# Moving 25 zero writes behind the load they stood ahead of, and six to another queue, in the last attention of a decode-step kernel

## The chip, the cores and the metric

The kernel runs on one core of a Trainium2 chip. HBM is the chip's main memory, SBUF the core's working memory; DMA transfers between them are issued by an engine's queue (SyncE's or GpSimd's here), and TensorE, VectorE and ScalarE compute. The time is the device time of one execution in microseconds (us), lower is better. Times below are medians of all executions of a kernel. Profile times count from the start of the profiled span, which is about 2 us shorter than the time of the same execution.

## The reference, cut to what matters

The program is the forward pass of attention, MLP, attention, MLP for one token, and its gradient (`jax.vjp`) for every input. Both attentions share their weights and KV cache, and so do both MLPs. Attention looks only at the last W = 4096 of 32768 cache rows:

```python
k = jnp.repeat(k_cache[:, :, Sk - W:, :], rep, axis=1)
v = jnp.repeat(v_cache[:, :, Sk - W:, :], rep, axis=1)
...
x = x + _A_ref(_layernorm(x), k_cache, v_cache, wq, wo)      # "A1"
x = x + _B_ref(_layernorm(x), w1, b1, w2)                    # "B2"
x = x + _A_ref(_layernorm(x), k_cache, v_cache, wq, wo)      # "A3"
x = x + _B_ref(_layernorm(x), w1, b1, w2)                    # "B4"
```

So the gradients of the two caches are zero in 28672 of 32768 rows. These zeros, 2 x 4 x 28672 x 128 values of two bytes, 58.7 MB, have to be written to HBM by the kernel; it does so in 112 writes of 512 KB. They depend on nothing and can go out at any time. A third of the 172 MB that the kernel moves are these zeros, and they are the kernel's filling material: put where the DMA would be idle, they are free.

## The kernel before: the parts that matter

The zero writes go out from SyncE's queue (`zeros`) or from GpSimd's (`bg_zeros`, which first copies one column of a named tile so that the writes don't start too early):

```python
def zeros(n):
    for _ in range(min(n, len(zero_jobs))):
        nc.sync.dma_start(zero_jobs.pop(0), zt[:])

def bg_zeros(n, after):
    if n:
        nc.gpsimd.tensor_copy(gate_t[:], after[:, 0:1])
    for _ in range(min(n, len(zero_jobs))):
        nc.gpsimd.dma_start(zero_jobs.pop(0), zt[:])
```

Of the 16 chunks of wo, nine are kept in SBUF and seven are streamed through NB = 6 buffers. All large loads go out from SyncE. The backward pass of an attention (`first` is true for A3, false for A1, the last attention to be differentiated) starts like this:

```python
def attn_bwd(g_col, g_bf, lname, sv, first, nxt):
    ...
    for c in range(NR, min(NO, NR + NB)):
        held[c] = wo_load(c)                    # six streamed chunks
    if first:
        bg_zeros(Z["A3c"], g_bf)
    else:
        zeros(Z["A1"])                          # 29 zero writes, SyncE
    late = list(range(NR, NO))
    ...                                         # (kept chunks; uses g_bf)
    def T(i):
        c = late[i]
        if c not in held:
            held[c] = wo_load(c)                # the seventh: needs a buffer back
        w = held[c]
        xpose(*nat_blocks(w[:, 1, :]), "a")     # 8 TensorE transposes, ScalarE copy
        nc.vector.tensor_tensor_reduce(...)     # VectorE: the chunk's other half
    def M(i, _):                                # 8 matmuls on chunk i
        ...
        if not first and i:
            nextprep()                          # small side jobs (GpSimd, TensorE)
    pipe(list(range(len(late))), T, M)
    if first:
        pre.extend(w2_load(c) for c in range(NB))
        bg_zeros(Z["A3d"], g_bf)
        fill(100, ["V"])
    else:
        after_stream()
    ...  # serial chain: do_p (dO), dP, dS, dq, the product with wq, layer norm
```

One of the side jobs writes the gradient of b1 out, and its row lies in the single buffer `kp`; the next user of that buffer is the copy `yr` of the row sums at the end of the serial chain:

```python
def rows_copy(bank, eng):
    yr = work.tile([P, 512], FP32, name="yr", tag="kp")
    ...
def db1_out():
    ...
    db_row = work.tile([NW2, P, 2], BF16, name="db_row", tag="kp", ...)
    ...
    nc.gpsimd.dma_start(out_7.rearrange(...), db_row[:]...)
```

The final stage computes the weight and cache gradients as outer products, 40 MB of writes from SyncE, with the remaining zeros strewn in:

```python
Z = dict(B2=3, A3=16, B4=[5, 2, 1, 2, 1, 2, 6], A3c=6, A3d=29, W1=3, A1=29)
...
run(6)
while jobs:
    zeros(1)
    run(9)
zeros(1000)
```

Of the kernel before, what the change touches and what calls it, by code (L numbers as in the profile page):

```python
# [23 lines left out]
def kernel(  # L24
# [102 lines left out]
# [3 lines that stand above are left out]
# [3 lines left out]
# [6 lines that stand above are left out]
# [120 lines left out]
    def fill(n, keys, how=None, six=False):  # L259
        for i in range(n):  # L260
            for k in keys:
                if xq[k]:
                    ap = xq[k].pop(0)
                    xpose(*nat_blocks(ap), None if how is None else how[i % len(how)], six)
                    break

    def level():
        ev[:] = [0.0, 0.0]
# [61 lines left out]
    def wo_load(c):  # L330
        if c < NR:
            w = wo_kept[c]
        else:
            w = strm.tile([P, 2, D], BF16, name="wo_c", tag="st")[:]
        nc.sync.dma_start(w, wo_v[c])
        return w

    def w2_load(c):
        w = strm.tile([P, 2, D], BF16, name="w2_c", tag="st")
        nc.sync.dma_start(w[:], w2_v[c])  # L340
        return w
# [25 lines left out]
    def pipe(items, T, M, lag=1):  # L367
        n = len(items)
        for i in range(n + lag):
            if i < n:  # L370
                T(items[i])
            if i >= lag:
                M(items[i - lag], i - lag)
# [46 lines left out]
    def attn_fwd(x_col, lname, first):  # L420
# [31 lines left out]
        if not first:  # L452
            for c in range(NR, min(NO, NR + NB)):
                held[c] = wo_load(c)
            bg_zeros(Z["A3"], n_bf)
            for w in wq_t:
# [130 lines left out]
    def w2_pass(a_bf, g_bf, x_col, xname, wgname, gbc, zn):  # L587

        acc = wide(TD + NW2)
        wg = keep.tile([P, NW2, 2], FP32, name=wgname)  # L590
        held = []

        def bwd1(w, c):
            for dch in range(TD):
                mv(acc, TD + c, w[:, 1, dch * P:(dch + 1) * P], g_bf[:, dch:dch + 1], False, dch == TD - 1)

        for c in range(NW2):
            w = pre.pop(0) if pre else w2_load(c)
            fwd_rows2(acc, w, c, a_bf, c == 0, c == NW2 - 1)
            ps = psum1([P, 8, P], BF16, "tps")  # L600
            for b in range(TD):
                nc.tensor.transpose(ps[:, b, :], w[:, 1, b * P:(b + 1) * P], ident_bf[:])  # L602
            nc.scalar.copy(w[:, 1, :], ps[:].rearrange("p b c -> p (b c)"))  # L603
            scr = work.tile([P, D], BF16, name="scr", tag="kp")
            nc.vector.tensor_tensor_reduce(out=scr[:], in0=w[:, 0, :], in1=gbc[:], scale=1.0, scalar=0.0,  # L605
                                           op0=ALU.mult, op1=ALU.add, accum_out=wg[:, c, 0:1])
            if held:
                bwd1(held.pop(), c - 1)
            if c == NW2 - 2 and zn:
                bg_zeros(zn, wg[:, c, :])  # L610
            held.append(w)
        bwd1(held.pop(), NW2 - 1)
        x_new = keep.tile([P, TD], FP32, name=xname)
        nc.vector.tensor_add(x_new[:], x_col[:], acc.cols(0, TD))
        nc.vector.tensor_copy(wg[:, :, 1:2], acc.cols(TD, TD + NW2)[:, :, None])
        return x_new, wg

    def mlp_fwd(x_col, lname, g_bf):
# [20 lines left out]
        sv["dact"] = dact  # L639
        x_new, wg = w2_pass(a_bf, g_bf, x_col, f"x_{lname}", "wg4", gbc, Z["B2"])  # L640
        return x_new, sv, wg
# [5 lines left out]
    def w1_block(b, hh):  # L647
        w = strm.tile([P, HT, CB], BF16, name="w1_b", tag="st")
        nc.sync.dma_start(w[:], w1_v[:, hh * HT:(hh + 1) * HT, b * CB:(b + 1) * CB])
        return w  # L650

    def mlp_turn(x_col, lname, wg, g_col, nxt):
# [22 lines left out]
        def lo0(b):  # L675
            return max(b - 1, 0) * FB
# [6 lines left out]
        for b in range(NBK):  # L683
            bg_zeros(Z["B4"][b], dh_bf[:, lo0(b):] if b else n_bf)
            ws[b] = [w1_block(b, hh) for hh in range(2)]
# [38 lines left out]
    def mlp_bwd_w1(g_col, lname, sv, nxt):  # L724
# [15 lines left out]
        level()  # L740
        bg_zeros(Z["W1"], sv["dh_bf"])
        pipe(list(range(2 * TD)), T, M)
        return ln_bwd(nacc.cols(0, TD), sv["n32"], sv["rstd"], g_col, lname, nxt)

    def attn_bwd(g_col, g_bf, lname, sv, first, nxt):
# [3 lines left out]
        held = {}  # L749
        for c in range(NR, min(NO, NR + NB)):  # L750
            held[c] = wo_load(c)
        if first:
            bg_zeros(Z["A3c"], g_bf)
        else:
            zeros(Z["A1"])
        late = list(range(NR, NO))
        gbc = bcast_row(g_bf)
        drow = sm_tile(P, 512)
# [42 lines left out]
# [3 lines that stand above are left out]
            fill(100, ["V"])  # L804
        else:
            after_stream()

        do_p = work.tile([P, 2, NO], BF16, name="do_p")
        dcols = dacc.cols(0, HQ).rearrange("p (c t) -> p t c", t=2)
# [242 lines left out]
    def after_stream():  # L1052
        slots.extend(strm.tile([P, 2048], BF16, name="st_o", tag="st")[:] for _ in range(NB))
# [9 lines left out]
        for _ in range(min(n, len(prep))):  # L1063
            prep.pop(0)()

    Z = dict(B2=3, A3=16, B4=[5, 2, 1, 2, 1, 2, 6], A3c=6, A3d=29, W1=3, A1=29)


    x1 = None
# [39 lines left out]
    x3, sA3 = attn_fwd(x2, "A3", False)  # L1109
    g3, g3b, sB4 = mlp_turn(x3, "B4", wg4, gcol, "A3")  # L1110
    g2, g2b = attn_bwd(g3, g3b, "A3", sA3, True, "B2")
    x4, wg2 = w2_pass(sB4["a_bf"], g2b, x3, "x_B4", "wg2", bcast_row(g2b), 0)
    dh_of(wg2, "B2", sB2)
# [4 lines left out]
    def db1_out():  # L1118
# [7 lines left out]
        nc.gpsimd.dma_start(out_7.rearrange("(c x) -> c x", x=2 * P), db_row[:].rearrange("c p t -> c (p t)"))  # L1126

    g0, g0b = attn_bwd(g1, g1b, "A1", sA1, False, "X0")
    level()
    nextprep(100)  # L1130
# [50 lines left out]
```

## Time and profile before

| | kernel before |
|---|---|
| time, median of the first 3 runs | 483.97 us (483.75 to 491.44) |
| span of the profiled run | 486.7 us |
| bytes moved | 172.23 MB, mean 354 GB/s |
| VectorE, ScalarE, TensorE busy | 49%, 46%, 67% |

The page cuts the span into 40 slices of 12.2 us. The rows are the granted TensorE clock in tenths (the share of full speed that the chip's throttle let TensorE run at), the busy share of the 16 DMA engines in tenths, and what they moved.

```profile
PEclk9996555587869998957987598855557555755555
DMA  8999999999999999999979999999000999999997
GB/s 328 387 415 419 407 370 383 342 359 392 413 375 396 350 307 377 415 417 417 414 291 310 329 342 339 416 420 417 26 1 3 393 413 403 413 413 409 421 415 301
```

The DMA is the limit nearly everywhere, but for three slices (26, 1 and 3 GB/s) in which it does nothing. The windows view, in microseconds, shows what stands on either side of that hole (columns: busy time and count for each engine, then granted clock, DMA share, GB/s):

```profile
310.00:320.00 10.00, 3.50 (x70) 2.96 (x67) 0.00 (x0) 6.20 (x8) 2.80 (x18) 0.85 1.03 417
320.00:330.00 10.00, 0.00 (x0) 0.00 (x0) 0.00 (x0) 0.00 (x0) 0.00 (x0) 0.50 1.03 421
330.00:340.00 10.00, 0.00 (x0) 0.00 (x0) 0.00 (x0) 0.00 (x0) 0.00 (x0) 0.50 1.02 419
345.00:376.00 31.00, 21.85 (x309) 12.63 (x309) 11.06 (x43) 7.16 (x11) 3.38 (x16) 0.67 0.01 2
```

First the DMA works for over 20 us while every engine is idle; then the engines work for 31 us while the DMA is idle. Two things that don't depend on each other run one after the other. (A DMA share of 1.03 is this view's full.) SyncE's queue in the timeline shows what ties them together (start, duration, queue, line, what, count):

```profile
299.33 32.66 SPq L129 DMA_DIRECT2D out_dram<-zt  x29
332.96 0.34 SPq L335 DMA_DIRECT2D wo_c<-in_A_wo_dram  x1
376.75 2.58 SPq L991 DMA_DIRECT2D out_dram<-wo_b  x3
```

and TensorE's and VectorE's first instructions after the hole say what they waited for, in brackets:

```profile
342.90 1.03 PE L186 MATMUL tps<-ident_bf,wo_c 128*128 128x128 bf16 x8 [28.15 <-DMA wo_c<-in_A_wo_dram]
343.02 1.22 DVE L784 CUSTOM_DVE_ANT_0 wo_c<-wo_c,gbc 128x1024 bf16<-128x1024 bf16 x1 [33.20 <-DMA wo_c<-in_A_wo_dram]
```

The seventh load was issued at 332.96 and landed 9.9 us later. Its buffer had been free since 308.8, when the last matmul that reads the old content ended,

```profile
308.45 0.36 PE L222 MATMUL acc<-gA_pair,wo_c 128*128 128x16 bf16 x8 [0.70 <-ACT wo_c L148]
```

but SyncE was working through the 29 zero writes that stand ahead of it in program order. The chain of waits, followed back from the end of the span, runs through just this:

```profile
311.85 0.96 SPq L129
...
312.85 10.05 DMA out_dram<-zt
...
322.92 9.97 DMA out_dram<-zt
...
332.96 9.89 DMA wo_c<-in_A_wo_dram
...
342.90 1.05 PE tps L186 x8
```

The last lines to keep for later are from the end of the serial chain, where the b1 row goes out and `yr` is copied:

```profile
367.86 0.51 POOL L1126 DMA_DIRECT2D out_dram<-db_row  x1 [12.38 <-DVE db_row L1125]
...
369.49 0.40 PE L222 MATMUL acc<-wq_b,dq_pair 128*32 128x512 bf16 x4
369.94 0.69 DVE L238 COPY yr<-acc 128x512 f32<-128x512 f32 x1 [2.38 <-PE acc L222]
370.69 1.05 PE L222 MATMUL sm<-sel,yr 128*128 128x2 f32 x8 [0.80 <-DVE yr L238]
```

The row lands in 1.6 us here, by the DMA view, and `yr` waits for TensorE alone.

### The profile page before, as it was taken

Reading aid. Unit: us, or ns where it says so; the run is one execution under the profiler, and the core shown is the slowest. Engines: PE = TensorE matmul, PEld = TensorE weight load, DVE = VectorE, ACT = ScalarE, POOL = GpSimd, SP = SyncE. Lnnn points to the kernel's source line nnn. Section 1 sums busy time; section 2 is a strip of 40 time slices with the busy share of each in tenths; the row PEclk is TensorE's granted clock in tenths of the full one; section 3 lists DMA queues with packets and bytes.
Section 4 is the critical chain, followed back from the end, with each engine's and each line's share of the span. In section 5 each row is a group of like instructions: output and inputs, shape, how many; then the busy total and the mean of one; then the engine's idle time right before and its main releaser. Section 6 shows DMA issues by size and latency. Waiting matters only on the chain.

```text
span 486.7 us, 11887 instructions
## 1 busy us (share of the span) xinstructions
PE 323.9 (67%) x5080; PEld 222.1 (46%) x5080; DVE 236.7 (49%) x489; ACT 225.3 (46%) x262; POOL 56.3 (12%) x145
## 2 busy tenths in 40 slices
PE   0566664887979888678977886700585857788600
PEld 0334343873769887557867885400352111111100
DVE  2224020873327665632667455400325988999900
ACT  1131100461518777635826452700232988999900
POOL 2000000014303123323400200400101000000000
PEclk9996555587869998957987598855557555755555
DMA  8999999999999999999979999999000999999997
GB/s 328 387 415 419 407 370 383 342 359 392 413 375 396 350 307 377 415 417 417 414 291 310 329 342 339 416 420 417 26 1 3 393 413 403 413 413 409 421 415 301
DMA packets 52256, 172.23 MB, mean 354 GB/s; under 512 B 5200, under 2 KB 12396, under 8 KB 51180
## 3 DMA queue, kind: packets, MB, share of 16 engines
q1 hardware_dynamic: 41120, 131.61, 70.1%
q0 software_dynamic: 11040, 39.86, 20.6%
q8 instruction: 39, 0.64, 0.5%
q14 instruction: 13, 0.11, 0.1%
q10 hardware_dynamic: 44, 0.01, 0.0%
HBM read 72.89 MB, written 98.58 MB: 352 GB/s over the span
## 4 chain that ended last, share of the span: by engine, by line
PE 18%; DMA 17%; ACT 10%; issue 4%; DVE 3%; SPq 3%; DVEq 0%; POOL 0%; ACTq 0%; POOLq 0%
PE tps L186 6%; ACT wq_b L148 5%; DMA w_c<-in_B_w_dram 4%; DMA out_dram<-zt 4%; DMA wo_c<-in_A_wo_dram 4%; PE acc L222 4%; PE ops L222 3%; SPq L129 3%; DMA out_dram<-wo_b 2%; DMA out_dram<-st_o 2%; PE d L222 1%; PE tps L602 1%; ACT st_o L148 1%; DMA out_dram<-wq_b 1%; ACT wo_b L148 1%
## 5 line engine op out<-in xcount | busy, mean ns | idle before, releaser
L222 PEld LDWEIGHTS <-w_c 128*128 128x128 bf16 x1120 | 36.5, 101 | 21.0 <-DMA w_c<-in_B_w_dram 14.3
L138 POOL DMA_DIRECT2D out_dram<-zt x76 | 40.7, 538 | 43.1 <-DMA out_dram<-zt 40.5
L603 ACT COPY w_c<-tps 128x1024 bf16<-128x1024 bf16 x28 | 28.3, 1012 | 25.4 <-PE tps L602 14.1
L222 PE MATMUL ops<-V 2*128 2x512 bf16 (+1 forms) x160 | 34.0, 588 | 6.5 <-ACT wq_b L148 3.5
L605 DVE CUSTOM_DVE_ANT_0 scr<-w_c,gbc 128x1024 bf16<-128x1024 bf16 x28 | 34.2, 1221 | 7.3 <-DMA w_c<-in_B_w_dram 5.3
L784 DVE CUSTOM_DVE_ANT_0 wo_c<-wo_c,gbc 128x1024 bf16<-128x1024 bf16 x14 | 16.3, 1217 | 40.6 <-DMA wo_c<-in_A_wo_dram 38.5
L145 DVE CAST wq_b<-ops 128x1024 bf16<-128x1024 f32 (+1 forms) x31 | 33.9, 1148 | 3.8 <-PE ops L222 3.2
L148 ACT CAST wq_b<-ops 128x1024 bf16<-128x1024 f32 (+1 forms) x33 | 33.8, 1141 | 2.2 <-PE ops L222 2.0
L148 ACT COPY K<-tps 128x1024 bf16<-128x1024 bf16 x19 | 18.8, 1017 | 30.9 <-PE tps L186 30.9
L222 PE MATMUL ops<-wo_b 2*128 2x512 bf16 x120 | 23.3, 567 | 10.9 <-ACT wq_b L148 7.2
L186 PE MATMUL tps<-ident_bf,wo_c 128*128 128x128 bf16 x112 | 9.1, 233 | 31.2 <-DMA wo_c<-in_A_wo_dram 31.2
L148 ACT COPY wo_c<-tps 128x1024 bf16<-128x1024 bf16 x14 | 14.0, 1026 | 30.9 <-PE tps L186 30.6
L222 PEld LDWEIGHTS <-V 128*128 128x128 bf16 (+2 forms) x416 | 14.0, 101 | 27.6 <-issue 27.6
L222 PE MATMUL q<-wq_b,nA_pair 128*32 128x512 bf16 x128 | 12.0, 461 | 18.0 <-DMA wq_b<-in_A_wq_dram 16.6
L602 PE MATMUL tps<-ident_bf,w_c 128*128 128x128 bf16 x224 | 22.5, 262 | 0.0
L186 PEld LDWEIGHTS <-wo_c 128*128 128x128 bf16 x112 | 7.2, 104 | 32.7 <-DMA wo_c<-in_A_wo_dram 31.5
L148 ACT COPY w_b<-tps 128x1024 bf16<-128x1024 bf16 x20 | 19.5, 1015 | 5.3 <-PE tps L186 4.9
L145 DVE COPY K<-tps 128x1024 bf16<-128x1024 bf16 x13 | 8.8, 690 | 25.9 <-PE tps L186 24.1
L186 PE MATMUL tps<-ident_bf,K 128*128 128x128 bf16 x256 | 21.0, 245 | 0.0
L186 PEld LDWEIGHTS <-K 128*128 128x128 bf16 x256 | 17.9, 111 | 3.4 <-issue 3.3
L222 PE MATMUL acc<-a_pair,w_c 128*128 128x16 bf16 x448 | 15.9, 172 | 5.2 <-DMA w_c<-in_B_w_dram 3.8
L186 PE MATMUL tps<-ident_bf,w_c 128*128 128x128 bf16 x224 | 17.3, 238 | 2.9 <-DMA w_c<-in_B_w_dram 2.9
(321 smaller groups left out, 659.4 us busy)
## 6 DMA issues: line engine op xcount, KB each, us to landing
out_dram<-zt POOLq DMA_DIRECT2D x76, 512.0 KB, 10.2
out_dram<-zt SPq DMA_DIRECT2D x36, 512.0 KB, 9.8
wo_c<-in_A_wo_dram SPq DMA_DIRECT2D x28, 512.0 KB, 8.3
w_c<-in_B_w_dram SPq DMA_DIRECT2D x32, 448.0 KB, 5.9
w_c<-in_B_w_dram SPq DMA_DIRECT2D x28, 512.0 KB, 6.7
out_dram<-wq_b SPq DMA_DIRECT2D x17, 512.0 KB, 10.5
wq_b<-in_A_wq_dram SPq DMA_DIRECT2D x16, 512.0 KB, 11.5
out_dram<-K SPq DMA_DIRECT2D x8, 1024.0 KB, 10.6
```

Source lines behind the costliest of these rows:

```text
L129: nc.sync.dma_start(zero_jobs.pop(0), zt[:])
L138: nc.gpsimd.dma_start(zero_jobs.pop(0), zt[:])
L145: nc.vector.tensor_copy(out_ap, in_ap)
L148: nc.scalar.copy(out_ap, in_ap)
L186: nc.tensor.transpose(ps[:, b, :], ap, ident_bf[:])
L222: nc.tensor.matmul(out_ap, lhsT=lhsT, rhs=rhs, start=start, stop=stop, skip_group_check=True, **kw)
L602: nc.tensor.transpose(ps[:, b, :], w[:, 1, b * P:(b + 1) * P], ident_bf[:])
L603: nc.scalar.copy(w[:, 1, :], ps[:].rearrange("p b c -> p (b c)"))
L605: nc.vector.tensor_tensor_reduce(out=scr[:], in0=w[:, 0, :], in1=gbc[:], scale=1.0, scalar=0.0, op0=ALU.mult, op1=ALU.add, accum_out=wg[:, ...
L784: nc.vector.tensor_tensor_reduce(out=w[:, 0, :], in0=w[:, 0, :], in1=gbc[:], scale=1.0, scalar=0.0, op0=ALU.mult, op1=ALU.add, accum_out=w ...
```

## The change

Its intent: let the seventh load pass the zeros, so that the zeros move under the serial chain. Six zeros go out on GpSimd's queue ahead of the load, to keep the DMA busy until the load's buffer comes free; 25 go out on SyncE behind it. The final stage is left with 5 zeros instead of 7.

```diff
@@ attn_bwd
-        if first:
-            bg_zeros(Z["A3c"], g_bf)
-        else:
-            zeros(Z["A1"])
+        bg_zeros(Z["A3c" if first else "A1c"], g_bf)
@@ after the streamed chunks
         else:
             after_stream()
+            zeros(Z["A1d"])
@@
-    Z = dict(B2=3, A3=16, B4=[5, 2, 1, 2, 1, 2, 6], A3c=6, A3d=29, W1=3, A1=29)
+    Z = dict(B2=3, A3=16, B4=[5, 2, 1, 2, 1, 2, 6], A3c=6, A3d=29, W1=3, A1c=6, A1d=25)
```

## The prediction

> What bounds the kernel now. Nearly everywhere the DMA engines are full: the 40-slice row shows DMA at 0.9 or more in most slices, at 410 to 420 GB/s for large writes. The exception is the last attention's backward part: the windows view gives a DMA share of 0.01 and 2 GB/s from 345 to 376 us. The timeline and the chain of waits say why. SyncE's queue issues 29 zero writes from 299.33 to 331.99 us, one per 1.0 to 1.2 us once some 8 are under way, and only then, at 332.96, the load of the seventh streamed wo chunk, which lands 9.9 us later (342.90). TensorE has run out of work at 315.2 and waits 28.15 us for it, VectorE 33.20 us. Its buffer was free long before: the last matmul that reads its old content ends at 308.8. From 342.9 a serial chain of 31.8 us (dO to layer norm) runs with nothing for the DMA to move, until the first outer products at 374.7 and the first output write at 376.75. After that the DMA is full (1.00 from 376 to 461), and writes drain for 24 us after the last compute: the final stage is DMA-bound.
>
> What the change does (instruction comparison). SyncE issues 7 wo loads in a row, then 25 zero writes; GpSimd issues a gate copy and 6 zero writes before its memset; the final stage keeps 5 of its 7 zero writes. Matmuls, casts and bytes are unchanged.
>
> Costs.
> - GpSimd: 0.2 us gate plus 6 zero writes (in the third layer the same six took 3.48 us). It starts near 301.0, when the gradient is cast, and ends near 304.8; its memset was waiting for TensorE until 306.76 anyway. No cost.
> - The load can issue at about 308.9. About 2 MB of GpSimd's zeros are then still moving; the Trainium skill, "DMA: Bandwidth & Descriptors", section "Queues, rings and completion order", says each engine alternates between queues by packet, so the load shares instead of standing behind them. The same arrangement in the third layer took 7.9 us from issue (200.4) to landing. I estimate 5 to 8 us: landing at 314 to 317.
> - Chain: TensorE reaches this chunk at about 315, so nearly the whole 28 us wait goes. The 31.8 us chain then ends near 347, first output write near 349.
> - DMA: a 512 KB zero takes 1.25 us of all engines (420 GB/s). 31 zeros and the load are 40 us from about 305.5, so they end near 346. Idle DMA shrinks from 33 us to about 3 us: the zeros hide under the chain instead of ahead of it.
> - Final stage: two zeros fewer, 2 x 1.25 = 2.5 us off a DMA-bound stage.
>
> Sum: 27.5 + 2.5 = 30 us, all on the critical path (DMA balance: 33 us idle less 3). 484 - 30 = 454 us. Losing all idle DMA time would give about 451. Range 450 to 461. Chances: faster by over 2% 0.97, within 2% 0.02, slower 0.01.
>
> What would show it. The load issues at 308 to 310 and lands by 317; TensorE's wait for it drops to under 4 us; 25 zeros issue from about 309 to 336; DMA share in the serial chain rises from 0.01 to above 0.8; first output write at 347 to 351; the final stage 2 to 3 us shorter.
>
> What would make it wrong. Zeros from two queues could slow the wo chunks; GpSimd could be held up over its six writes, delaying its memset and the transposes behind it; the chain of matmuls could run slower beside a full DMA or at another granted clock (0.50 to 0.76 there now); the final stage could become bound by its casts (VectorE and ScalarE busy 94% of it), losing the 2.5 us.

## The result, and the profile after

| | before | after |
|---|---|---|
| time, median of 4 runs each | 485.38 us (483.75 to 491.44) | 457.95 us (456.39 to 460.12) |
| span of the profiled run | 486.7 us | 455.4 us |
| mean DMA rate over the span | 354 GB/s | 378 GB/s |

The ratio is 0.9449, with a 95% interval of 0.9384 to 0.9514. Without the slow run of 491.44 us the median before is 483.97 us, and the gain is 26.0 us instead of 27.4. Ratios here and below are the mean time of one kernel's fast runs over the mean of the other's in the same rounds, so not quite the ratio of the medians quoted.

The same three rows of the page, now with slices of 11.4 us:

```profile
PEclk9997565577777989996798779977675555555555
DMA  7999999989999999999999899999973999999997
GB/s 318 365 411 426 407 407 342 410 298 334 416 416 382 402 322 331 389 417 417 417 414 410 311 347 359 375 394 415 415 324 137 406 415 402 415 413 409 420 413 308
```

The hole of three slices has shrunk to a dent of two (324 and 137 GB/s). SyncE's queue, and GpSimd's:

```profile
303.96 0.33 SPq L335 DMA_DIRECT2D wo_c<-in_A_wo_dram  x1
304.34 29.85 SPq L129 DMA_DIRECT2D out_dram<-zt  x25
```

```profile
296.36 3.15 POOL L138 DMA_DIRECT2D out_dram<-zt  x6
301.47 1.80 POOL L1045 MEMSET wo_b<- 128x2048 bf16 x1 [1.96 <-PE sm L222]
```

GpSimd issued its six in 3.15 us and then still waited 1.96 us for TensorE before its memset, so they cost it nothing. The load was issued as soon as its buffer was free and landed 5.6 us later. TensorE no longer waits for it (no bracket), VectorE 5.20 us, off the critical path:

```profile
309.67 0.61 PE L186 MATMUL tps<-ident_bf,wo_c 128*128 128x128 bf16 x8
309.74 1.22 DVE L781 CUSTOM_DVE_ANT_0 wo_c<-wo_c,gbc 128x1024 bf16<-128x1024 bf16 x1 [5.20 <-DMA wo_c<-in_A_wo_dram]
```

The windows view: engines and DMA now work at the same time, up to 338 us, and then there are 9.9 us of nearly idle DMA before the first output write at 348.38.

```profile
312.30:338.00 25.70, 19.79 (x289) 11.02 (x289) 8.16 (x33) 5.63 (x9) 2.23 (x11) 0.67 1.03 417
338.50:348.40 9.90, 4.06 (x23) 2.79 (x24) 3.59 (x11) 1.58 (x3) 0.52 (x1) 0.59 0.07 29
```

That is more than the 3 us that had been predicted. The end of the serial chain shows a wait that was not there before:

```profile
335.95 0.51 POOL L1124 DMA_DIRECT2D out_dram<-db_row  x1 [13.07 <-DVE db_row L1123]
...
337.58 0.40 PE L222 MATMUL acc<-wq_b,dq_pair 128*32 128x512 bf16 x4
...
340.76 0.69 DVE L238 COPY yr<-acc 128x512 f32<-128x512 f32 x1 [5.10 <-DMA out_dram<-db_row]
341.50 1.86 PE L222 MATMUL sm<-sel,yr 128*128 128x2 f32 x8 [3.52 <-DVE yr L238]
```

TensorE's sums were ready at 337.98, but `yr` was copied at 340.76, 2.8 us later (0.05 us in the kernel before), because its buffer still held the b1 row, whose write landed 4.7 us after its issue instead of 1.6. The chain of waits now goes through that write:

```profile
335.95 4.69 DMA out_dram<-db_row
...
340.76 0.70 DVE yr L238
...
341.50 1.88 PE sm L222 x8
```

One trap in comparing the two traces: the spans differ by 31.3 us, the fast medians by 26.0. The program ahead of the change is the same, yet the gradient that opens this stage (`gA_pair`) is ready at 300.76 us in one trace and at 295.48 in the other; over all traces it lies between 293.8 and 300.8, whatever the kernel. So the table counts from that mark, gA. The next marks are VectorE's first copy into `do_p`, with which the serial chain begins, the copy `yr` of the row sums, and the last gradient of the chain (`gX_pair`). The marks are starts of instructions, read from the timelines; idle DMA is the length from `gA` to the first output write times the missing part of the DMA share, (1.03 - share) / 1.03.

| run | gA to do_p | do_p to yr | yr to last gradient | gA to first output write | idle DMA in it | first output write to end | b1 row lands in |
|---|---|---|---|---|---|---|---|
| before | 45.64 | 23.54 | 3.97 | 75.99 | 36.2 | 109.9 | 1.6 |
| after | 18.02 | 27.26 | 4.77 | 52.90 | 9.8 | 107.0 | 4.7 |

By these, the change gives 23.1 us up to the first output write and 2.9 us after it, together 26.0, as in the fast medians.

### The profile page after: what moved, and what is told of

It reads as the page before. It is cut to its first block, busy times and chain, and to the rows that moved or that the text cites. A ratio compares the mean times of both kernels' runs of the same rounds, so it can differ in the third digit from the quotient of the medians.

```text
span 455.4 us, 11888 instructions
## 1 busy us (share of the span) xinstructions
PE 326.9 (72%) x5080; PEld 222.8 (49%) x5080; DVE 236.8 (52%) x489; ACT 224.9 (49%) x262; POOL 60.5 (13%) x152
## 3 DMA queue, kind: packets, MB, share of 16 engines
q0 software_dynamic: 11904, 43.01, 23.5%
## 4 chain that ended last, share of the span: by engine, by line
PE 21%; ACT 12%; DMA 11%; issue 4%; DVE 3%; DVEq 0%; POOL 0%; ACTq 0%; SPq 0%; POOLq 0%
PE tps L186 7%; ACT wq_b L148 6%; DMA w_c<-in_B_w_dram 5%; PE ops L222 5%; PE acc L222 4%; DMA out_dram<-st_o 2%; ACT wo_b L148 2%; PE sm L222 2%; ACT st_o L148 2%; DMA wo_c<-in_A_wo_dram 2%; PE d L222 2%; DMA out_dram<-wq_b 1%; ACT wo_c L148 1%; ACT V L148 1%; DMA out_dram<-db_row 1%
## 5 line engine op out<-in xcount | busy, mean ns | idle before, releaser
L138 POOL DMA_DIRECT2D out_dram<-zt x82 | 44.3, 543 | 47.2 <-DMA out_dram<-zt 44.7
L222 PE MATMUL q<-wq_b,nA_pair 128*32 128x512 bf16 x128 | 14.2, 554 | 16.7 <-DMA wq_b<-in_A_wq_dram 15.3
L186 PE MATMUL tps<-ident_bf,K 128*128 128x128 bf16 x256 | 22.0, 251 | 0.2 <-ACT K L148 0.2
L602 PE MATMUL tps<-ident_bf,w_c 128*128 128x128 bf16 x224 | 21.3, 253 | 0.0
L222 PEld LDWEIGHTS <-wo_b 2*128 2x128 bf16 (+1 forms) x152 | 5.7, 101 | 29.3 <-issue 28.6
L148 ACT CAST K<-ops 128x1024 bf16<-128x1024 f32 x18 | 17.5, 1014 | 2.6 <-PE ops L222 2.1
L186 PE MATMUL tps<-ident_bf,w_c 128*128 128x128 bf16 x224 | 17.3, 238 | 1.9 <-DMA w_c<-in_B_w_dram 1.9
L186 PE MATMUL tps<-ident_bf,wq_b 128*128 128x128 bf16 x256 | 18.0, 237 | 0.4 <-issue 0.4
```

Of the source, the lines that this page charges most:

```text
L148: nc.scalar.copy(out_ap, in_ap)
L186: nc.tensor.transpose(ps[:, b, :], ap, ident_bf[:])
L222: nc.tensor.matmul(out_ap, lhsT=lhsT, rhs=rhs, start=start, stop=stop, skip_group_check=True, **kw)
L602: nc.tensor.transpose(ps[:, b, :], w[:, 1, b * P:(b + 1) * P], ident_bf[:])
```

## The experiments

Eleven runs were made, on three chips; each shares its runs of the kernel before (medians 485.18, 484.84 and 486.04 us), so kernels are best compared by their ratios. "Changed" in the diffs below is the changed kernel.

| run | edit to the changed kernel | median us | ratio to before (95%) |
|---|---|---|---|
| after_again | none | 457.87 | 0.9454 (0.9411 to 0.9497) |
| sync31 | all 31 zeros on SyncE, behind the load | 457.79 (fast runs 456.66) | 0.9437 (0.9396 to 0.9478) |
| ownrow | b1 row in a buffer of its own | 454.89 | 0.9384 (0.9336 to 0.9431) |
| zeros30 | 30 zeros behind the load, none in the final stage | 452.17 | 0.9325 (0.9294 to 0.9356) |
| oldorder | the 25 ahead of the load again | 485.34 | 1.0024 (0.9966 to 1.0081) |
| zeros30_ownrow | both edits | 449.40 | 0.9280 (0.9237 to 0.9323) |
| nozeros | no zeros in this stage | 492.62 | 1.0157 (1.0090 to 1.0223) |
| sync36_ownrow | as zeros30_ownrow, all 36 on SyncE | 457.71 | 0.9425 (0.9375 to 0.9474) |
| best_again | zeros30_ownrow, second timing | 450.83 | 0.9294 (0.9256 to 0.9332) |
| sync36_again | sync36_ownrow, second timing | 456.87 | 0.9403 (0.9368 to 0.9437) |
| before_ownrow | (kernel before) b1 row in its own buffer | 485.53 | 1.0011 (0.9961 to 1.0060) |

Every run matched the reference. The marks, as above:

| run | gA to do_p | do_p to yr | yr to last gradient | gA to first output write | idle DMA in it | first output write to end | b1 row lands in |
|---|---|---|---|---|---|---|---|
| after_again | 17.50 | 26.87 | 4.77 | 51.98 | 8.6 | 107.0 | 5.0 |
| sync31 | 16.92 | 27.14 | 4.78 | 51.68 | 8.0 | 107.4 | 5.5 |
| ownrow | 18.58 | 23.71 | 4.57 | 49.70 | 6.3 | 107.0 | 5.0 |
| zeros30 | 18.01 | 27.24 | 4.77 | 52.86 | 3.6 | 102.9 | 6.9 |
| oldorder | 49.32 | 24.46 | 3.76 | 80.38 | 37.5 | 107.1 | 1.6 |
| zeros30_ownrow | 18.03 | 24.48 | 3.75 | 49.10 | 0.5 | 102.9 | 5.6 |
| nozeros | 16.96 | 23.75 | 3.96 | 47.53 | 42.9 | 146.0 | 1.6 |
| sync36_ownrow | 16.71 | 23.73 | 4.49 | 49.53 | 5.3 | 108.1 | 5.4 |
| best_again | 18.12 | 23.76 | 4.52 | 49.25 | 0.5 | 103.0 | 5.6 |
| sync36_again | 18.02 | 22.25 | 4.65 | 50.41 | 7.8 | 108.3 | 5.7 |
| before_ownrow | 45.43 | 23.70 | 3.97 | 75.95 | 35.4 | 109.9 | 1.6 |

### after_again: the changed kernel beside its variants

No edit.

> The changed kernel unaltered, timed in the same rounds as the three variants. Expected 457 to 459 us as on record, and the same marks: the seventh wo load lands 5 to 6 us after its issue, the copy of the row sums (yr) waits about 5 us, 3 of them for the landing of the db1 row, about 10 us of idle DMA before the first output write. Both theories below agree here; it also shows how much the stretch ahead of the change wanders from run to run (the two traces differ by 5.3 us there).

As expected: 457.87 us, the wait for the b1 row is there again (5.0 us to landing, `yr` 26.87 us after do_p). The load took 6.9 us to land this time, a little over the 5 to 6 expected, and TensorE waited 1.11 us for it.

### oldorder: the same split, but the zeros ahead of the load

```diff
         bg_zeros(Z["A3c" if first else "A1c"], g_bf)
+        if not first:
+            zeros(Z["A1d"])
@@
             after_stream()
-            zeros(Z["A1d"])
```

> The changed kernel's split (6 zeros on GpSimd, 25 on SyncE, 5 in the final stage), but with the 25 ahead of the seventh load, as in the kernel before. Theory A (only the order matters): the load still stands behind 25 zeros, TensorE waits some 25 to 30 us for it, the DMA idles 30 us in the serial chain; 481 to 485 us, at most the 2.5 us of the two zeros that the final stage loses faster than before. Rival B (the second queue lets the load through, or carries a part of the gain by itself): under 475 us.

485.34 us, the time of the kernel before. GpSimd sends its six, SyncE its 25, and the load stands behind these 25:

```profile
294.81 36.33 SPq L129 DMA_DIRECT2D out_dram<-zt  x25
332.11 0.34 SPq L335 DMA_DIRECT2D wo_c<-in_A_wo_dram  x1
```

```profile
342.06 1.03 PE L186 MATMUL tps<-ident_bf,wo_c 128*128 128x128 bf16 x8 [32.52 <-DMA wo_c<-in_A_wo_dram]
```

TensorE waits 32.52 us, the whole gain is gone. The time is 0.3 us above the 481 to 485 us expected: do_p comes 3.7 us later than in the kernel before (49.32 against 45.64 us after gA), with 31 zeros instead of 29 moving ahead of the load's data (two more are 2.5 us), and the final stage gives 2.8 us of that back. So neither the second queue nor the two zeros taken out of the final stage explains the change's time; the order of the load and the zeros does.

### sync31: the right order, but nothing on GpSimd

```diff
-  A1c=6, A1d=25
+  A1c=0, A1d=31
```

> All 31 zeros of this stage on SyncE behind the seventh load, none on GpSimd. Theory A (the order of the load against the zeros is the whole gain; the six on GpSimd only fill a gap ahead of the load, and there are 10 us of idle DMA to spare later): same time as the changed kernel within 2 us, load lands in 3 to 5 us, the zeros end 3 to 5 us later in the stage, so the db1 row may land later and cost up to 3 us. Rival B (the second queue itself carries part of the gain): 4 to 8 us slower than the changed kernel.

457.79 us (456.66 without the slow run), against 457.87 for the changed kernel in the same rounds. So no worth of the six zeros on GpSimd shows in the changed kernel; the intervals of the two ratios leave room for some 3 us either way. The load lands faster without them, in 4.5 us, and the DMA has less to do while SyncE's queue waits for the load's buffer:

```profile
290.00:310.00 20.00, 14.12 (x248) 10.52 (x245) 11.17 (x24) 11.36 (x14) 6.31 (x31) 0.91 0.71 265
```

A share of 0.71 over 20 us is about 6 us of idle DMA, (1.03 - 0.71) / 1.03 x 20. In the changed kernel the six zeros fill that, but since about 9 us of DMA are idle later, it makes no difference which of the two gaps they lie in: idle DMA from gA to the first output write is 8.0 us here and 8.6 to 9.8 us there.

### ownrow: the b1 row in another buffer

```diff
-  db_row = work.tile([NW2, P, 2], BF16, name="db_row", tag="kp", padded_shape=[NW2, WC // 2, 2])
+  db_row = work.tile([NW2, P, 2], BF16, name="db_row", tag="rw5", padded_shape=[HQ, P, 2])
```

The buffer `rw5` was last read well before, so no wait is taken away that data needs; instructions and their order stay the same on every engine.

> The db1 row gets another buffer, so that the copy of the row sums need not wait for its write to land. Theory A (the shortfall against the predicted 454 us is this new wait: the row landed in 4.7 us instead of 1.6 us because zeros fill the DMA): the wait of 5.1 us falls to about 2 us (for TensorE), the chain gets 2.8 us shorter, up to 3.6 us if the fp32 matmuls behind it no longer run at the lower granted clock; 454 to 455.5 us. Rival B (the shortfall is a slower serial chain beside a full DMA): no change in time.

454.89 us, 3.0 us less. The two intervals overlap, since the runs of one kernel scatter by 5 to 7 us, but the trace shows the mechanism: the row still takes 5.0 us to land, and nobody waits for it.

```profile
342.38 0.69 DVE L238 COPY yr<-acc 128x512 f32<-128x512 f32 x1 [2.43 <-issue]
```

do_p to `yr` falls from 27.26 and 26.87 us (the two traces of the changed kernel) to 23.71 us. That is the 23.54 us of the kernel before, where the DMA was idle. In these two traces of the changed kernel `yr` came 2.8 and 3.1 us after TensorE's sums; here it came 0.1 us after them. So the wait for the row was most of the shortfall, and no slowing of the chain by a full DMA shows. The same edit on zeros30 (zeros30_ownrow below) gave 2.8 us. It was run on another chip. What was not as expected: the eight fp32 matmuls after `yr` took 1.66 us, at a granted clock of 0.58, still above the 1.05 us (clock 0.94) of the kernel before.

### before_ownrow: the same edit in the kernel before

The same diff, in the kernel before.

> The kernel before with the db1 row in a buffer of its own. If the wait for that row was made by the change (in the kernel before the DMA is idle at that point and the row lands in 1.6 us, ahead of the end of TensorE's work), nothing changes: same time within 1.5 us. If the shared buffer costs something in any case, 2.5 to 3.5 us faster, as in the changed kernel.

485.53 us, ratio 1.0011: nothing changes, and do_p to `yr` is 23.70 us. The shared buffer was harmless until the change put a full DMA beside it.

### zeros30: all remaining zeros behind the load

```diff
-  A1c=6, A1d=25
+  A1c=6, A1d=30
```

> 30 instead of 25 zeros behind the load, none left for the final stage. Final stage shorter by 5 x 1.25 = 6.25 us in all theories. Theory A (the small db1 row waits behind all zeros under way at its issue): it lands 8 to 10 us after its issue, the chain gets 3 to 5 us longer, net 1 to 3 us faster than the changed kernel. Theory B (the engines alternate between the two queues, so the row's landing doesn't depend on how many zeros are queued): it lands in about 5 us, net 5 to 6 us faster.

452.17 us, 5.7 us less than the changed kernel. Neither theory's landing time came: the b1 row landed in 6.9 us, longer than the 4.7 and 5.0 us of the changed kernel, but shorter than 8 to 10. The net is that of theory B, though `yr` now waited longer for the row:

```profile
342.36 0.69 DVE L238 COPY yr<-acc 128x512 f32<-128x512 f32 x1 [7.36 <-DMA out_dram<-db_row]
```

It was copied 5.0 us after TensorE's sums, against 2.8 and 3.1 in the changed kernel. In this trace the sums themselves came sooner (22.2 us after do_p, against 24.5 and 23.8), so do_p to `yr` did not grow. The landing thus grows with what is queued, but what sets it is left open. In the final stage the five zeros are worth 4.1 us, not 6.25: in the next run, which also has none there, the DMA runs dry for about 2 us (share 0.83 from 380 to 390 us), where SyncE had no output ready from 378.5 to 382.34.

### zeros30_ownrow and best_again: both edits

Both diffs above.

> Both edits that helped: 30 zeros behind the load, none in the final stage, and the db1 row in a buffer of its own. The zeros30 run still had about 3.5 us of idle DMA ahead of the first output write. If the wait for the row's landing is what opens it, the chain gets 3 us shorter and the idle DMA nearly vanishes: 449 to 450 us, against 452.2 us. If the granted clock or the chain is slower beside a full DMA, 451 to 452 us.

> A second timing of the best version, in the same rounds as a second timing of sync36_ownrow: 449 to 451 us, beginning of the last gradient stage to first output write near 49 us.

449.40 and 450.83 us, 0.9280 and 0.9294 of the kernel before, 1.7 to 1.8% below the changed kernel (0.9454), as expected. Idle DMA ahead of the first output write is down to 0.5 us. This is the best version. The windows view of the first of the two at the load:

```profile
290.00:300.00 10.00, 6.48 (x102) 4.31 (x100) 5.82 (x15) 1.39 (x2) 3.72 (x7) 0.83 1.00 387
300.00:310.00 10.00, 6.73 (x127) 5.75 (x124) 4.41 (x9) 9.26 (x11) 5.78 (x27) 0.98 1.02 385
```

### sync36_ownrow and sync36_again: the best version without GpSimd's six

```diff
-  A1c=6, A1d=30
+  A1c=0, A1d=36
```

> As zeros30_ownrow, but all 36 zeros on SyncE behind the load. In the sync31 run the DMA share from 300 to 310 us was 0.69, so about 3 us went idle there, and 8 to 10 us of idle DMA later took that up. Here no idle DMA is left later, so if that reading is right the six zeros on GpSimd are now worth 2 to 4 us: 451.5 to 453.5 us. If GpSimd's six are worth nothing in any case, the same as zeros30_ownrow within 1 us.

> The first timing was 8.3 us over zeros30_ownrow, more than the 2 to 4 us expected; its profile (span 452.2 against 447.0 us) shows only 5.2 us, with about 5.3 us of idle DMA between 290 and 310 us. If the gap ahead of the load is all of it, 454 to 456 us here, 5 to 6 us over best_again; if 8 us come again, some other cost of the missing GpSimd zeros must be found.

457.71 us, 8.3 us over the best version, where 2 to 4 were expected. The direction is right, the size was not: the expectation had looked only at the window from 300 to 310 us, and the idle DMA begins before it.

```profile
290.00:300.00 10.00, 7.30 (x128) 5.18 (x126) 6.74 (x15) 1.89 (x3) 0.32 (x1) 0.83 0.75 282
300.00:310.00 10.00, 6.94 (x138) 5.90 (x135) 4.87 (x10) 9.90 (x13) 6.10 (x31) 1.00 0.72 254
```

Together (1.03 - 0.75 + 1.03 - 0.72) / 1.03 x 10 = 5.7 us. The second timing gave 456.87 us, 6.0 us over best_again (the expectation had 5 to 6, and 454 to 456 us), and its trace has 7.8 us of idle DMA against 0.5. So the gap ahead of the load accounts for 5 to 7 us, and the six zeros that were worth nothing in the changed kernel are worth 6 us here. What the first timing's remaining 2 us were was not pursued; by the ratios, which use means, the two differences are 7.0 and 5.3 us.

### nozeros: no zeros in this stage at all

```diff
-  A1c=6, A1d=25
+  A1c=0, A1d=0
```

> No zeros in this stage at all; 36 go out at the very end. Theory A (31 zeros are hidden under the serial chain, so they cost nothing there; the final stage is DMA-bound at 1.25 us for each): the final stage is 31 x 1.25 = 39 us longer, the db1 row lands in under 2 us and the chain is 2 to 3 us shorter: 493 to 497 us. Rival (the chain runs slower because the DMA is full beside it): the chain gets shorter by clearly more than 3 us, so under 492 us.

492.62 us, just under the 493 to 497 expected. The final stage is 146.0 - 107.0 = 39.0 us longer for 31 more zeros, 1.26 us each, as expected. The chain is 5.4 us shorter (gA to first output write 47.53 against 52.90): 3.5 us of it between do_p and `yr`, 0.8 after `yr`, and 1.1 before do_p, where the load lands in 3.4 instead of 5.6 us. That is more than the 2 to 3 us expected of theory A, and by its length alone it meets the rival's mark of clearly more than 3 us; the time lies between the two forecasts. The trace says where it comes from: 2.7 us are the wait for the row, and in the rest no serial chain slowed by the full DMA shows. do_p to `yr`, 23.75 us, is that of ownrow (23.71) and of the best version's second trace (23.76), which have a full DMA beside them. (Over the nine traces without a wait for the row this figure wanders from 22.25 to 24.48 us; oldorder has 24.46 with an idle DMA beside it, sync36_again 22.25 with a full one.)

## Why the prediction was right, point by point

- **What bounded the kernel, and the mechanism: right.** Order alone accounts for the gain: oldorder loses all of it, sync31 keeps all of it.
- **The load: right.** Predicted to issue at about 308.9 and to land in 5 to 8 us; with the start of the stage 5.3 us earlier it issued at 303.96, and landed in 5.6 us (6.9 in a second trace). The Trainium skill, "DMA: Bandwidth & Descriptors", section "Queues, rings and completion order", says that an engine takes turns between queues by packet. The traces agree that zeros of the other queue slow the load: with GpSimd's six under way it took 5.6 to 7.4 us, without them 3.4 to 4.8 us. No run here shows whether the engines took turns by packet or finished what was left of the six first: the last of the six landed at 308.1 us in the changed kernel, the load at 309.6, and one 512 KB transfer is 1.25 us. do_p came 18.02 us after gA; the prediction's figures give 18.1 (346.4 - 27.5 - 300.8).
- **GpSimd: right.** No cost; it waited for TensorE after its six writes.
- **The serial chain: the step that failed.** The prediction took its 31.8 us over unchanged: "The 31.8 us chain then ends near 347, first output write near 349", that is about 48 us after gA. It was 52.90. Of the 4.5 us that the chain grew after do_p, 3.7 lie before `yr`. Of these, 2.7 are the new wait for the b1 row's buffer (`yr` came 2.8 us after TensorE's sums instead of 0.05), which ownrow takes away. The other 1.0 is that the sums came later (24.5 us after do_p, against 23.5): two groups of matmuls took 3.60 and 1.44 us instead of 3.27 and 0.84, at a granted clock of 0.50 and 0.55 instead of 0.57 and 0.96. That is no mark of a full DMA, since oldorder, with an idle DMA, has its sums 24.4 us after do_p. The prediction had listed matmuls at another granted clock among its doubts, but not that a small write of the same stage would land later once the DMA is full, and that something waits for it.

  The remaining 0.8 us are the eight fp32 matmuls after `yr`: 1.86 us at a granted clock of 0.50, instead of 1.05 us at 0.94 in the kernel before. In all four traces in which TensorE had to wait for the b1 row (3.5 to 5.8 us ahead of these matmuls) the clock in them was 0.50; in the nine others, which waited under 1 us, it was 0.55 to 1.00, so the wait may have cost this too, but a lower clock also came without it (1.66 us at 0.58 in ownrow).
- **The first output write: a mark met by luck.** It came at 348.38 us, inside the forecast 347 to 351, but only because the stage began 5.3 us earlier in this trace than in the one the forecast was worked out from. Counted from gA, the forecast is 46 to 50 us, and 52.90 missed it.
- **The zeros' end and the idle DMA: mis-sized as a consequence.** Predicted 3 us of idle DMA, measured 9.8: the first output write came 4.7 us later, and the zeros ended 1 to 2 us earlier than worked out (the DMA share falls to 0.31 between 339 and 340 us, which is 44 us after gA; predicted 45).
- **The final stage: right.** Two zeros fewer gave 2.9 us, predicted 2.5. The Trainium skill's "DMA: Bandwidth & Descriptors", section "Where 436 GB/s comes from", says that the HBM side, about 358 GB/s, binds for transfers between HBM and SBUF; its section "Measured (HBM→SBUF, 128 partitions, SWDGE, issued from GpSimd)" ties that figure to both cores of an HBM domain streaming. This kernel has one core, and its zero writes ran at 417 to 421 GB/s, so the 1.25 us from the trace was the figure to use, and nozeros confirms it with 1.26 us.
- **The total.** Predicted 454 us within 450 to 461; measured 457.95. The gain was 26.0 us between fast medians instead of 30 (23.1 and 2.9 in the traces, for 27.5 and 2.5). With the new wait taken away the time is 454.89 us.

## What to carry to other kernels

Where a load waits behind bulk writes in one queue, ask what the load feeds: if the work that it feeds leaves the DMA idle, the bulk can move behind the load and hide there, as nearly all of it did here. Once a stretch of idle DMA is filled, look at every small transfer in it whose landing something waits for, a buffer's next user above all, since its time to land is no longer that of an idle DMA. And a filler that shows no worth while there is other slack (the six zeros in the changed kernel) can be worth 6 us once that slack is used up, so test it again at the end.

## What the Trainium skill lacked or had wrong

- "DMA: Bandwidth & Descriptors", section "Issuing engines are not separate DMA queues": it says that issuing from several engines saves only the time it takes to initiate the DMA. The page's section "Anatomy of one DMA — SWDGE (gpsimd) path" adds that a semaphore wait happens on the issuing sequencer, before dispatch. What the page doesn't draw from this is that one DMA that waits for its buffer holds up those behind it in the program order of its queue, so that a second queue can be worth more than issue time: with nothing on GpSimd's queue 5.7 us of DMA went idle in that way, and the six zeros there were worth 6.0 to 8.3 us once no other slack was left.
- The same page, section "Latency and other measured facts": it says that an HBM access takes 0.2 us on average and 2 us at high load, and that a lighter load makes the fixed cost smaller, but not how long a small write takes beside a stream that fills the core's own DMA engines. A write of 7 KB landed in 1.6 us beside idle engines and in 4.7 to 6.9 us beside a stream of 512 KB writes from another queue. What sets that time was not settled.
- The same page, section "Where 436 GB/s comes from": about 358 GB/s is named as what binds between HBM and SBUF, without the condition (both cores streaming) that stands in another section of the page. Taken alone the sentence is too low for this kernel: long streams of SBUF to HBM writes on one core ran at 417 to 421 GB/s.
